# Sparse attention with an ELU MLP on one core: batch 2 transposed by the DMA crossbar, and batch 0's local P v moved ahead of its strided half

## The chip, the core and the metric

The kernel runs on one core of one Trainium2 chip. The metric is device time in microseconds (us) of one execution. "Before" names the kernel as it stood, "after" the changed one. Line numbers (L12) are those of the kernel before.

## The reference, cut to what matters

```python
# q, k, v: (8 batches, 8 heads, 576 positions, 64) f32
scores = q @ k.T / sqrt(64)
local   = (rel >= 0) & (rel < 32)                  # heads 0-3, rel = query - key
strided = (rel >= 0) & (pos_k % 32 == pos_q % 32)  # heads 4-7
attn = softmax(where(mask, scores, -1e9))          # then / (sum + 1e-9)
y = attn @ v                                       # (8, 8, 576, 64)
x = y.transpose(0, 2, 1, 3).reshape(4608, 512)
h = x @ w_in                                       # (512, 2048)
g = where(h > 0, h, exp(min(h, 0)) - 1)            # ELU
out = g @ w_out                                    # (2048, 512)
```

## The kernel before, in words

**Attention.** The eight heads of a batch are taken in four pairs: pairs 0 and 1 have the local mask, 2 and 3 the strided one. The positions are renumbered so that the strided mask falls into small blocks; each pair is worked in two halves (u = 0, 1). The steps of a pair and half have letters, which the item lists of the code use:

- T, `piece_T` (L255): transposes of q and k of the pair on TensorE into PSUM, then one copy each to SBUF (L253) on VectorE or ScalarE. The results lie in qlT and klT (local) and qsT and ksT (strided), each with two buffers, for even and odd batches.
- S, `piece_S` (L274): scores (L293), exp on ScalarE (L296), product with the mask on VectorE (L298 strided, L304 local), which gives pm.
- M, `mm_O2` (L355): the sums of pm (L368, L374) and P v (L378).
- E, `tail_O2` (L382): 1/sum as ln and exp on ScalarE (L385, L387), and the product into xT on VectorE (L313, L317). X is M and E together; O is a variant for later batches (L339).

**MLP.** The 4608 rows are taken in 18 subtiles of 256. `l1` (L397) makes hps = x w_in for two of 16 column blocks (L406), then the ELU: exp on ScalarE (L413), then two VectorE steps (L420, L421), or Relu on ScalarE and one VectorE step (L416, L417). `l1_wide` (L423) does four blocks at once (L431, L437, L439, L440). `l2` (L457) makes a quarter of a 128-row output (L463); after the fourth, ScalarE copies it out (L468) and SP stores it.

**Order.** The program is scheduled by hand: each engine runs its instructions in the order in which they are written. `spins` (L487) are idle matmuls, about 0.145 us each, that stand between TensorE's steps in the head of the kernel. The stages:

1. Batch 0's attention, with f32 loads and casts on the engines, by an item list (L530-555). The order before is: local T and S; strided transposes T2, T3; strided S4 to S7; strided M4 to M7; local M0 to M3; 12 spins. `cast_v` (L156) casts the local v; `one_columns` (L525) fills the columns of ones in vlx and vsx, on ScalarE, in two places (item "1", and after the list).
2. L1 of subtiles 0 and 1 (L576-582), first `l1_wide` (hpw), with batch 1's strided transposes T2, T3 between.
3. L2 of those subtiles, with the rest of batch 1's attention between its 16 quarters (item list L602-625, "2" is one quarter). Item "t" there transposes batch 2's strided pairs, on TensorE.
4. The main loop (L655-663): step n is one `l1` of the subtiles 2 to 17, and `l2` runs on so far that n + 10 quarters are done. The remaining attention is hung in at given n. SC[b] gives the n at which the S steps of a batch start, in the order of pairs 2, 3, 0, 1; its X or O follow 1.5 steps later. Batch 2's local transposes are at n = 8 and 10 ("TT").

From batch 3 on, the four transposes of a batch are done by DMA (`dma_T` L161, "Ts"), issued by SP, each a single instruction of all four heads, with rows padded from 72 to 80. Batches 1 and 2 are transposed on TensorE; for them `load_ql16` (L112) brings q in one DMA in a layout (qld) that is transposed in 16 pieces of 64 rows (L268) in place of 8 of 128.

**Loads.** The loads of batch 0's local q and k are issued by SP and ScalarE; all others by Pool, one after another, in the order written. `load_str` (L141) fills qs, ks or vs; these three have one buffer each, so that a load of the next batch waits until all of the previous one has been read.

Of the kernel before, what the change touches and what calls it, by code (L numbers as in the profile page):

```python
# [17 lines left out]
D = 64  # L18
HG = 4
NS = 8  # L20
RS = S // NS
LQ = 96
LB = S // LQ
PRE = STRIDE
SUB = 256
RP = 80
# [4 lines left out]
def kernel(  # L31
# [44 lines left out]
    vs = const([RS, HG, NS * D], BF16, "vs")  # L76

    qlb = [const([RP, 2, NS, 2 * D], BF16, f"qlb{i}") for i in range(2)]
    qld = [t.rearrange("p a s c -> p (a s c)").rearrange("p (h c) -> p h c", h=HG) for t in qlb]
    klb = [const([LQ, 2, LB, 2 * D], BF16, f"klb{i}") for i in range(2)]  # L80
    KLW = PRE + 2 * S
    KSW = 16 * RP + 48
# [23 lines left out]
    def load_vl(b, eng):  # L106
        x = v[b, 0:HG].rearrange("h (t p) d -> p (h t) d", p=LQ)
        t = vl32.rearrange("p a x t d -> p (a x t) d")
        eng.dma_start(out=t[PRE:128], in_=x)
        eng.dma_start(out=t[0:PRE, 1:], in_=x[LQ - PRE:, 0:HG * LB - 1, :])  # L110


    def load_ql16(b):
        if b < 3:
            nc.gpsimd.dma_start(out=qld[b % 2][0:RS],
                                in_=q[b, 0:HG].rearrange("h (p s) d -> p h (s d)", s=NS))
            return
        for h in range(HG):
            nc.gpsimd.dma_start(  # L119
                out=qlb[b % 2][0:RS, h // 2, :, (h % 2) * D:(h % 2 + 1) * D],  # L120
                in_=q[b, h].rearrange("(p s) d -> p s d", s=NS))

    def load_kl16(b):
        for h in range(HG):
            nc.gpsimd.dma_start(  # L125
                out=klb[b % 2][:, h // 2, :, (h % 2) * D:(h % 2 + 1) * D],
                in_=k[b, h].rearrange("(t p) d -> p t d", p=LQ))
# [14 lines left out]
    def load_str(b, dst, src):  # L142
        nc.gpsimd.dma_start(  # L143
            out=dst[0:RS], in_=src[b, HG:2 * HG].rearrange("h (p s) d -> p h (s d)", s=NS))
# [35 lines left out]
    ones = const([128, D], BF16, "ones")  # L180
    dist = const([RS, RS], I32, "dist")
    nc.vector.memset(warm, 1.0)  # L182
    nc.vector.memset(identity, 1.0)
    nc.vector.memset(base_l, 1.0)
    for t in (qs, ks):
# [2 lines left out]
        identity, identity, compare_op=ALU.is_equal, fill=0.0,  # L188
        base=0, pattern=[[1, 128]], channel_multiplier=-1,
    )  # L190
    load_str(0, qs, q)
    load_str(0, ks, k)
    nc.gpsimd.affine_select(
        base_l, base_l, compare_op=ALU.is_ge, fill=0.0, base=-1,
        pattern=[[-1, NS], [-NS, LQ // NS]], channel_multiplier=1)
    nc.gpsimd.affine_select(
        base_l, base_l, compare_op=ALU.is_ge, fill=0.0, base=PRE,
        pattern=[[1, NS], [NS, LQ // NS]], channel_multiplier=-1)
    load_str(0, vs, v)
    nc.gpsimd.iota(dist, pattern=[[1, RS]], base=RS, channel_multiplier=-1)  # L200
    nc.vector.memset(qlb[0][64:RP], 0.0)
    load_vl(0, nc.gpsimd)
    for i in range(2):
        nc.gpsimd.dma_start(out=w_in_sb[i],
                            in_=w_in_v[:, :, i * 1024:(i + 1) * 1024])

    nc.vector.memset(vl32[0:PRE, 0, 0, 0, :], 0.0)
    nc.vector.memset(ones, 1.0)
    for i in range(2):
        nc.vector.memset(klT[i][:, 0:PRE], 0.0)  # L210
# [20 lines left out]


    def pitch(b):
        return RS if b < 3 else RP

    def t_parts(b, hp, nm):
        i, a, n = b % 2, hp % 2, RS
        if hp >= 2:
            src = qs if nm == "q" else ks
            dst = (qsT if nm == "q" else ksT)[i][:, a * 8 * n:(a + 1) * 8 * n]  # L240
            blk = [src[0:n, 2 * a + j // 4, (j % 4) * 128:(j % 4 + 1) * 128] for j in range(8)]
        elif nm == "q":
            dst = qlT[i][:, a * 8 * n:(a + 1) * 8 * n]
            blk = ([qlb[i][0:n, a, j] for j in range(NS)] if b not in (1, 2) else
                   [[qld[i][0:n, 2 * a + x, j * D:(j + 1) * D] for x in range(2)]
                    for j in range(NS)])
        else:
            dst = klT[i][:, PRE + a * S:PRE + (a + 1) * S]
            blk = [klb[i][:, a, j] for j in range(LB)]
        return dst, blk  # L250
# [4 lines left out]
    def piece_T(b, hp, engs=None, wide=True):  # L255
        both = [t_parts(b, hp, nm) for nm in "qk"]
        if wide:
            pw = p_x.tile([128, 2, 1024], BF16, tag="x", name="tp2")
            ps = [pw[:, 0, 0:S], pw[:, 1, 0:S]]
        else:  # L260
            ps = [p_h.tile([128, S], BF16, tag="h", name="tp") for _ in range(2)]
        for i, (dst, blk) in enumerate(both):
            n = S // len(blk)
            for j, x in enumerate(blk):
                o = ps[i][:, j * n:(j + 1) * n]
                if type(x) is list:
                    for z in range(2):
                        nc.tensor.transpose(o[z * D:(z + 1) * D], x[z], identity[0:n, 0:n])  # L268
                else:
                    nc.tensor.transpose(o, x, identity[0:n, 0:n])  # L270
        for i, (dst, blk) in enumerate(both):
            copy(engs[i] if engs else nc.vector, dst, ps[i])

# [248 lines left out]
    cast_q(nc.vector, 1)  # L522
    cast_k(nc.vector, 1)
    P = [(p, u) for p in range(4) for u in range(2)]
    def one_columns(i):  # L525
        for t in (vlx[i], vsx[i]):
            o = t.rearrange("p a t (y d) -> p (a t) y d", d=D)[:, :, 1, :]
            nc.scalar.copy(o, warm[0:o.shape[0], 0:D].unsqueeze(1).to_broadcast(o.shape))

    for it in ("f7 S0 S1 1 f6 T1 f6 S2 S3 m f8 T2 T3q T3k f3 S4 S5 f3 S6 S7 M4 f3 E4 M5 f3 E5 M6 f3 E6 "  # L530
               "v M7 f3 E7 M0 f3 E0 M1 f3 E1 M2 f3 E2 M3 f12 E3").split():
        n = int(it[1:].strip("qk")) if len(it) > 1 else 0
        if it == "m":
            mask_strided()
        elif it[0] == "f":
            spins(n)
        elif it == "1":
            one_columns(0)
        elif it == "v":
            cast_v(nc.vector, 0, 0)  # L540
            cast_v(nc.gpsimd, 0, 1)
        elif it[0] == "T" and len(it) == 3:
            dst, blk = t_parts(0, n, it[2])
            ps = p_h.tile([128, S], BF16, tag="h", name="tp")
            for j, x in enumerate(blk):
                nc.tensor.transpose(ps[:, j * RS:(j + 1) * RS], x, identity[0:RS, 0:RS])
            copy(nc.vector, dst, ps)
        elif it[0] == "T":
            piece_T(0, n, (nc.vector, nc.scalar if n > 1 else nc.vector), False)
        elif it[0] == "S":  # L550
            do(("S", 0, *P[n]))
        elif it[0] == "M":
            do(("M", 0, *P[n], p_h))
        else:
            do(("E", 0, *P[n]))

    nc.vector.memset(qlb[1][64:RP], 0.0)
    nc.vector.memset(vlx[1][0:PRE, :, 0, :], 0.0)
    one_columns(1)
    load_str(1, qs, q)  # L560
    load_str(1, ks, k)

# [19 lines left out]
            l1(j, 4 * h + 3)  # L582
    load_str(2, qs, q)
    load_str(2, ks, k)
    load_kl16(2)
    load_ql16(2)
    load_vl16(2)


    L2S = [(j, kk, part) for j in range(NSUB) for kk in range(2) for part in range(4)]  # L590
# [8 lines left out]
                l2_last(j, kk)  # L599
            l2n[0] += 1  # L600

    for it in ("2 S4 2 S5 2 2 B4 S6 2 E4 A5 S7 2 E5 B6 2 E6 A7 2 E7 v "  # L602
               "T0 2 S0 S1 2 T1 k B0 2 E0 S2 2 A1 E1 S3 2 B2 E2 2 A3 2 E3 t 2 x").split():
        n = int(it[-1]) if it[-1].isdigit() else 0
        if it == "2":
            l2_to(l2n[0] + 1)
        elif it == "v":
            load_str(2, vs, v)
        elif it == "k":
            load_kl16(3)  # L610
            load_ql16(3)
            load_vsx16(3)
        elif it == "t":
            for p in (2, 3):
                piece_T(2, p)
        elif it == "x":
            load_str(3, qs, q)
            load_str(3, ks, k)
            load_vl16(3)
        elif it[0] == "T":  # L620
            piece_T(1, n, (nc.vector, nc.scalar))
        elif it[0] in "AB":
            do(("M", 1, *P[n], p_x if it[0] == "A" else p_h))
        else:
            do((it[0], 1, *P[n]))
# [3 lines left out]
    def at(n, *its):  # L629
        jobs.setdefault(int(2 * n) / 2, []).extend(its)  # L630

    def Ts(b):
        for w in ("qs", "ks", "kl", "ql"):
            dma_T(b, w)


    SC = {2: (2.5, 5.5, 9, 12), }
    SC.update({b: tuple(15 + 16 * (b - 3) + 4 * i for i in range(4)) for b in range(3, B)})
    for p, n in ((0, 8), (1, 10)):
        at(n, lambda p=p: do(("TT", 2, p)))  # L640

    for b in range(3, B):
        st = int(SC[b][0])
        if b > 3:
            at(st - 13, lambda b=b: (load_str(b, qs, q), load_str(b, ks, k), load_kl16(b),
                                     load_ql16(b), load_vsx16(b), load_vl16(b)))
        at(st - (3 if b == 3 else 4), lambda b=b: Ts(b))
    for b in range(2, B):
        for i, p in enumerate((2, 3, 0, 1)):
            for u in range(2):  # L650
# [5 lines left out]
    for n, (j, t) in enumerate(L1S):  # L656
        for f in jobs.pop(n, []):
            f()
        l2_to(n + 10)
        for f in jobs.pop(n + .5, []):  # L660
            f()
        l1(j, t, mode="B" if n < 18 and n % 3 == 0 else "A")
# [31 lines left out]
```

The softmax here doesn't subtract the row's maximum and nothing guards it: scores larger than these inputs give would overflow.

## Time and profile before

| | before |
|---|---|
| time, median of 6 runs | 324.55 us |
| lowest and highest of the 6 | 323.82 and 326.07 us |
| the profiled execution, its own time | 324.17 us |
| its span in the profile | 322.5 us |
| PE (TensorE) busy | 310.7 us, 96% of the span |
| DVE (VectorE), ACT (ScalarE), Pool busy | 239.5, 220.2, 114.9 us |
| L463, L2 matmuls | 143.6 us |
| L406, L1 matmuls | 140.7 us |

The span is the stretch from the first to the last instruction; 324.17 - 322.5 = 1.7 us of the execution lie outside it. Busy time is a sum over instructions; an engine that is busy for 96% of the span can gain by less work or by smaller gaps. The chain of waits, which the profile follows back from the last instruction, tells for each moment which engine or transfer held up the end. PE is TensorE, PEld its weight loads, SP the engine that issues stores and DMA transposes.

### The profile page before, as it was taken

Reading aid. Unit: us, or ns where it says so; the run is one execution under the profiler, and the core shown is the slowest. Engines: PE = TensorE matmul, PEld = TensorE weight load, DVE = VectorE, ACT = ScalarE, POOL = GpSimd, SP = SyncE. Lnnn points to the kernel's source line nnn. Section 1 sums busy time; section 2 is a strip of 40 time slices with the busy share of each in tenths; the row PEclk is TensorE's granted clock in tenths of the full one; section 3 lists DMA queues with packets and bytes.
Section 4 is the critical chain, followed back from the end, with each engine's and each line's share of the span. In section 5 each row is a group of like instructions: output and inputs, shape, how many; then the busy total and the mean of one; then the engine's idle time right before and its main releaser. Section 6 shows DMA issues by size and latency. Waiting matters only on the chain.

```text
span 322.5 us, 7819 instructions
## 1 busy us (share of the span) xinstructions
PE 310.7 (96%) x2992; PEld 223.9 (69%) x2992; DVE 239.5 (74%) x485; ACT 220.2 (68%) x429; POOL 114.9 (36%) x162
## 2 busy tenths in 40 slices
PE   8898998979999999999999999999999999999995
PEld 6668944567667777777777777777777777777763
DVE  7764973477667888888888888898888866666660
ACT  3787765677788788777777777778788643443431
POOL 6262376896046903491269025920000000000000
PEclk9999999999999999999999999999999999999999
DMA  7999999999199939995999499969211111111212
GB/s 169 195 208 210 207 151 139 154 149 129 34 144 181 135 54 150 180 125 79 140 172 154 62 134 169 148 77 167 59 35 35 34 35 33 34 35 48 51 33 65
DMA packets 113990, 36.36 MB, mean 113 GB/s; under 512 B 101154, under 2 KB 107458, under 8 KB 113954
## 3 DMA queue, kind: packets, MB, share of 16 engines
q0 software_dynamic: 79696, 18.87, 60.9%
q1 hardware_dynamic: 32766, 16.28, 24.2%
q10 hardware_dynamic: 1492, 0.74, 0.9%
q8 instruction: 23, 0.38, 0.5%
q14 instruction: 13, 0.11, 0.1%
HBM read 38.04 MB, written 9.44 MB: 147 GB/s over the span
## 4 chain that ended last, share of the span: by engine, by line
PE 83%; DVE 6%; ACT 4%; DMA 4%; issue 1%; SPq 0%; DVEq 0%; ACTq 0%
PE ops L463 37%; PE hps L406 33%; PE sc L293 3%; PE ox L345 3%; DMA kl<-in_k_dram 2%; DVE g L421 2%; DMA ksT<-ks 1%; DVE he L420 1%; DVE g L440 1%; PE opl L478 1%; PE idle L487 1%; PE tp L270 1%; ACT big L437 1%; ACT wr L439 1%; PE o_ps L378 1%
## 5 line engine op out<-in xcount | busy, mean ns | idle before, releaser
L463 PE MATMUL ops<-w_out_sb,g 128*128 128x512 bf16 x560 | 143.6, 380 | 0.1
L406 PE MATMUL hps<-xT,w_in_sb 128*128 128x256 bf16 x1088 | 140.7, 273 | 1.3 <-DVE g L421 1.3
L406 PEld LDWEIGHTS <-w_in_sb 128*128 128x128 bf16 x1088 | 117.3, 114 | 23.6 <-issue 1.4
L413 ACT ACTIVATE he<-hps 128x512 f32<-128x512 f32 x136 | 80.2, 592 | 52.2 <-PE hps L406 50.4
L421 DVE TENSOR_TENSOR g<-he,hps 128x512 bf16<-128x512 bf16 x130 | 89.3, 687 | 13.5
L463 PEld LDWEIGHTS <-g 128*128 128x128 bf16 x560 | 50.4, 98 | 37.2 <-DVE g L421 0.3
L420 DVE TENSOR_SCALAR he<-he 128x512 bf16<-128x512 f32 x130 | 58.0, 446 | 20.9 <-ACT he L413 19.5
L296 ACT ACTIVATE e<-sc 128x576 bf16<-128x576 f32 (+1 forms) x64 | 38.4, 645 | 4.5 <-PE sc L293 4.4
L468 ACT COPY osb<-ops 128x512 f32<-128x512 f32 x35 | 20.5, 587 | 12.4 <-PE ops L463 9.7
L143 POOL DMA_DIRECT2D qs<-in_q_dram x8 | 6.1, 761 | 50.1 <-DMA qsT<-qs 48.9
L125 POOL DMA_DIRECT2D klb<-in_k_dram x28 | 20.7, 751 | 8.6 <-DMA w_in_sb<-in_moe_w_in_dram 4.5
L348 ACT ACTIVATE ln<-ox 64x288 f32<-64x288 f32 x40 | 16.3, 408 | 10.6 <-PE ox L345 10.1
L133 POOL DMA_DIRECT2D vlx<-in_v_dram x28 | 22.0, 785 | 4.3 <-DMA w_out_sb<-in_moe_w_out_dram 2.3
L317 DVE TENSOR_TENSOR xT<-ox,rc 64x288 bf16<-64x288 f32 x40 | 18.1, 453 | 5.7 <-ACT rc L351 5.3
L313 DVE TENSOR_TENSOR xT<-ox,rc 64x288 bf16<-64x288 f32 x40 | 18.1, 453 | 5.7 <-ACT rc L351 5.4
L119 POOL DMA_DIRECT2D qlb<-in_q_dram x20 | 16.5, 831 | 13.1 <-DMA ks<-in_k_dram 9.0
L134 POOL DMA_DIRECT2D vlx<-in_v_dram x28 | 17.3, 616 | 4.9 <-DMA qs<-in_q_dram 1.6
L351 ACT ACTIVATE rc<-ln 128x288 f32<-128x288 f32 x40 | 17.7, 443 | 1.3
L349 ACT ACTIVATE ln<-ox 64x288 f32<-64x288 f32 x40 | 16.1, 403 | 0.5
L138 POOL DMA_DIRECT2D vsx<-in_v_dram x20 | 16.2, 819 | 0.0
L304 DVE TENSOR_TENSOR pm<-e,mask_l 128x576 bf16<-128x576 bf16 x32 | 13.5, 452 | 3.5 <-ACT e L296 3.1
L487 PE MATMUL idle<-warm 128*128 128x256 bf16 x92 | 14.7, 306 | 1.3 <-DVE warm L182 1.3
(101 smaller groups left out, 242.8 us busy)
## 6 DMA issues: line engine op xcount, KB each, us to landing
out_dram<-osb SPq DMA_DIRECT2D x31, 144.0 KB
qs<-in_q_dram POOLq DMA_DIRECT2D x8, 288.0 KB, 6.7
ks<-in_k_dram POOLq DMA_DIRECT2D x8, 288.0 KB, 8.4
w_in_sb<-in_moe_w_in_dram POOLq DMA_DIRECT2D x2, 1024.0 KB, 15.9
w_out_sb<-in_moe_w_out_dram POOLq DMA_DIRECT2D x4, 512.0 KB, 16.4
klb<-in_k_dram POOLq DMA_DIRECT2D x28, 72.0 KB, 8.2
vlx<-in_v_dram POOLq DMA_DIRECT2D x28, 72.0 KB, 3.8
qlb<-in_q_dram POOLq DMA_DIRECT2D x20, 72.0 KB, 7.1
```

Of the source, the lines that this page charges most:

```text
L125: nc.gpsimd.dma_start(out=klb[b % 2][:, h // 2, :, (h % 2) * D:(h % 2 + 1) * D], in_=k[b, h].rearrange("(t p) d -> p t d", p=LQ))
L133: nc.gpsimd.dma_start(out=t[PRE:128], in_=x)
L296: nc.scalar.activation(e[0:R], sc[0:R, :, 0:W], ACT.Exp, scale=scale)
L313: nc.vector.tensor_mul(xs[:, u * W:(u + 1) * W], o[pr], rc[pr])
L317: nc.vector.tensor_mul(dst, o[pr].rearrange(pat, b=3, s=NS), rc[pr].rearrange(pat, b=3, s=NS))
L406: nc.tensor.matmul(hps[:, mm], lhsT=w_in_of(m, c), rhs=xT[:, c, r0:r0 + SUB], start=(c == 0), stop=(c == KC - 1))
L413: nc.scalar.activation(e, hps, ACT.Exp)
L420: eng.tensor_scalar(e1, e, scalar1=1.0, scalar2=1.0, op0=ALU.min, op1=ALU.subtract)
L421: nc.vector.tensor_tensor(gt, e1, hps, op=ALU.max)
L463: nc.tensor.matmul(ops, lhsT=g[:, m, kk * 128:(kk + 1) * 128], rhs=w_out_sb[:, m, :], start=(m == 0), stop=(m == MC - 1))
L468: nc.scalar.copy(o_sb, ops)
L487: nc.tensor.matmul(ps, lhsT=warm[:, 0:128], rhs=warm[:, 0:ps.shape[-1]], start=True, stop=True, skip_group_check=True)
```

## The change

1. **Batch 0, head.** The fills of ones go to the very start of ScalarE's work, the two memsets of v's first rows ahead of the others on VectorE. The load of the local v is Pool's first, ahead of qs; the load of ks follows the two `affine_select`. The item list takes the local P v (M0 to M3) before the strided transposes, with `cast_v` right after `mask_strided`; the strided halves run S4 S6 S5 S7 and M4 M6 M5 M7; the tail of 12 spins and E3 is gone. There are 81 spins in place of 92.
2. **Batches 1 and 2, q.** The qld layout is gone: `load_ql16` issues four DMAs of 72 KB for every batch.
3. **Batch 2.** Its four transposes are DMA transposes on SP: qs and ks at the first "t" of the item list of stage 3, kl and ql at the second. The TT steps are gone, and `pitch` is 80 for batch 2.
4. **Batch 2, later.** SC[2] is (4.5, 7.5, 10, 12.5) in place of (2.5, 5.5, 9, 12). Three of the 16 L2 quarters of stage 3 move into the first steps of the main loop.
5. **Batch 1.** T0 goes ahead of A7, both of its copies to VectorE. Pool's loads of batch 2 (kl, ql, vl) come after that of vs, at "v"; those of batch 3 are split between "k" and "x" in another order.

The diff, without the removed definitions of `one_columns` and `Ts`, which only move:

```diff
-qld = [t.rearrange("p a s c -> p (a s c)").rearrange("p (h c) -> p h c", h=HG) for t in qlb]
...
 def load_ql16(b):
-    if b < 3:
-        nc.gpsimd.dma_start(out=qld[b % 2][0:RS],
-                            in_=q[b, 0:HG].rearrange("h (p s) d -> p h (s d)", s=NS))
-        return
     for h in range(HG):
...
 nc.vector.memset(warm, 1.0)
+nc.vector.memset(vl32[0:PRE, 0, 0, 0, :], 0.0)
+nc.vector.memset(vlx[1][0:PRE, :, 0, :], 0.0)
...
+for i in range(2):
+    one_columns(i)
+load_vl(0, nc.gpsimd)
 load_str(0, qs, q)
-load_str(0, ks, k)
 nc.gpsimd.affine_select(
...
+load_str(0, ks, k)
 load_str(0, vs, v)
 nc.gpsimd.iota(dist, pattern=[[1, RS]], base=RS, channel_multiplier=-1)
 nc.vector.memset(qlb[0][64:RP], 0.0)
-load_vl(0, nc.gpsimd)
...
 def pitch(b):
-    return RS if b < 3 else RP
+    return RS if b < 2 else RP
...
-for it in ("f7 S0 S1 1 f6 T1 f6 S2 S3 m f8 T2 T3q T3k f3 S4 S5 f3 S6 S7 M4 f3 E4 M5 f3 E5 M6 f3 E6 "
-           "v M7 f3 E7 M0 f3 E0 M1 f3 E1 M2 f3 E2 M3 f12 E3").split():
+for it in ("f7 S0 S1 f6 T1 f6 S2 S3 m v f6 M0 f3 E0 M1 f3 E1 M2 f3 E2 M3 f3 T2 E3 T3q T3k f3 S4 S6 f3 S5 S7 "
+           "M4 f3 E4 M6 f3 E6 M5 f3 E5 M7 f3 E7").split():
...
-nc.vector.memset(vlx[1][0:PRE, :, 0, :], 0.0)
-one_columns(1)
 load_str(1, qs, q)
...
 load_str(2, ks, k)
-load_kl16(2)
-load_ql16(2)
-load_vl16(2)
...
-for it in ("2 S4 2 S5 2 2 B4 S6 2 E4 A5 S7 2 E5 B6 2 E6 A7 2 E7 v "
-           "T0 2 S0 S1 2 T1 k B0 2 E0 S2 2 A1 E1 S3 2 B2 E2 2 A3 2 E3 t 2 x").split():
+for it in ("2 S4 2 S5 2 2 B4 S6 2 E4 A5 S7 2 E5 B6 2 E6 T0 2 t A7 v E7 S0 2 T1 S1 2 k B0 2 E0 S2 2 A1 E1 S3 t B2 2 "
+           "E2 A3 E3 x").split():
...
     elif it == "v":
         load_str(2, vs, v)
+        load_kl16(2)
+        load_ql16(2)
+        load_vl16(2)
     elif it == "k":
+        load_str(3, qs, q)
+        load_str(3, ks, k)
+        load_vsx16(3)
         load_kl16(3)
         load_ql16(3)
-        load_vsx16(3)
     elif it == "t":
-        for p in (2, 3):
-            piece_T(2, p)
+        Ts(2, *(("qs", "ks") if l2n[0] < 10 else ("kl", "ql")))
     elif it == "x":
-        load_str(3, qs, q)
-        load_str(3, ks, k)
         load_vl16(3)
     elif it[0] == "T":
-        piece_T(1, n, (nc.vector, nc.scalar))
+        piece_T(1, n, (nc.vector, nc.scalar if n else nc.vector))
...
-SC = {2: (2.5, 5.5, 9, 12), }
+SC = {2: (4.5, 7.5, 10, 12.5), }
...
-for p, n in ((0, 8), (1, 10)):
-    at(n, lambda p=p: do(("TT", 2, p)))
...
-    l2_to(n + 10)
+    l2_to(max(n + 10, min(13 + (n + 2) // 2, 16)))
```

More of the change, by code (lines that the diff above doesn't have):

```diff
@@ L190, with one_columns @@
     )
+    def one_columns(i):
+        for t in (vlx[i], vsx[i]):
+            o = t.rearrange("p a t (y d) -> p (a t) y d", d=D)[:, :, 1, :]
+            nc.scalar.copy(o, warm[0:o.shape[0], 0:D].unsqueeze(1).to_broadcast(o.shape))
+    for i in range(2):
+        one_columns(i)
+    load_vl(0, nc.gpsimd)
     load_str(0, qs, q)
-    load_str(0, ks, k)
     nc.gpsimd.affine_select(
@@ L205 @@
                             in_=w_in_v[:, :, i * 1024:(i + 1) * 1024])
-    nc.vector.memset(vl32[0:PRE, 0, 0, 0, :], 0.0)
     nc.vector.memset(ones, 1.0)
@@ L243, in t_parts @@
             dst = qlT[i][:, a * 8 * n:(a + 1) * 8 * n]
-            blk = ([qlb[i][0:n, a, j] for j in range(NS)] if b not in (1, 2) else
-                   [[qld[i][0:n, 2 * a + x, j * D:(j + 1) * D] for x in range(2)]
-                    for j in range(NS)])
+            blk = [qlb[i][0:n, a, j] for j in range(NS)]
         else:
@@ L265, in piece_T @@
                 o = ps[i][:, j * n:(j + 1) * n]
[L266 to L270, printed above, removed]
+                nc.tensor.transpose(o, x, identity[0:n, 0:n])
         for i, (dst, blk) in enumerate(both):
@@ L524 @@
     P = [(p, u) for p in range(4) for u in range(2)]
[L525 to L528, printed above, removed]
-    for it in ("f7 S0 S1 1 f6 T1 f6 S2 S3 m f8 T2 T3q T3k f3 S4 S5 f3 S6 S7 M4 f3 E4 M5 f3 E5 M6 f3 E6 "
-               "v M7 f3 E7 M0 f3 E0 M1 f3 E1 M2 f3 E2 M3 f12 E3").split():
+    for it in ("f7 S0 S1 f6 T1 f6 S2 S3 m v f6 M0 f3 E0 M1 f3 E1 M2 f3 E2 M3 f3 T2 E3 T3q T3k f3 S4 S6 f3 S5 S7 "
+               "M4 f3 E4 M6 f3 E6 M5 f3 E5 M7 f3 E7").split():
         n = int(it[1:].strip("qk")) if len(it) > 1 else 0
@@ L536 @@
             spins(n)
-        elif it == "1":
-            one_columns(0)
         elif it == "v":
@@ L600, in l2_to, with Ts @@
             l2n[0] += 1
-    for it in ("2 S4 2 S5 2 2 B4 S6 2 E4 A5 S7 2 E5 B6 2 E6 A7 2 E7 v "
-               "T0 2 S0 S1 2 T1 k B0 2 E0 S2 2 A1 E1 S3 2 B2 E2 2 A3 2 E3 t 2 x").split():
+    def Ts(b, *names):
+        for w in names:
+            dma_T(b, w)
+    for it in ("2 S4 2 S5 2 2 B4 S6 2 E4 A5 S7 2 E5 B6 2 E6 T0 2 t A7 v E7 S0 2 T1 S1 2 k B0 2 E0 S2 2 A1 E1 S3 t B2 2 "
+               "E2 A3 E3 x").split():
         n = int(it[-1]) if it[-1].isdigit() else 0
@@ L630, in at @@
         jobs.setdefault(int(2 * n) / 2, []).extend(its)
-    def Ts(b):
-        for w in ("qs", "ks", "kl", "ql"):
-            dma_T(b, w)
-    SC = {2: (2.5, 5.5, 9, 12), }
+    SC = {2: (4.5, 7.5, 10, 12.5), }
     SC.update({b: tuple(15 + 16 * (b - 3) + 4 * i for i in range(4)) for b in range(3, B)})
-    for p, n in ((0, 8), (1, 10)):
-        at(n, lambda p=p: do(("TT", 2, p)))
     for b in range(3, B):
@@ L646 @@
                                      load_ql16(b), load_vsx16(b), load_vl16(b)))
-        at(st - (3 if b == 3 else 4), lambda b=b: Ts(b))
+        at(st - (3 if b == 3 else 4), lambda b=b: Ts(b, "qs", "ks", "kl", "ql"))
     for b in range(2, B):
```

## The prediction

> **What bounds the kernel now.** I read the page's busy times first, then the chain of waits in two windows, then PE's waits, then the rows of the DMA transposes. The page says that PE is busy nearly always, and its DMA row (40 slices of 8.06 us) that the DMA engines are full until about 81 us, with one lull in the eleventh slice:
>
> ```profile
> span 322.5 us, 7819 instructions
> PE 310.7 (96%) x2992; PEld 223.9 (69%) x2992; DVE 239.5 (74%) x485; ACT 220.2 (68%) x429; POOL 114.9 (36%) x162
> DMA  7999999999199939995999499969211111111212
> ```
>
> So the end moves only by what PE does, or by what PE waits for. From about 88 us on PE's waits are too small to matter; all that the change can do lies before that. The chain of waits in the head (start us, duration us, what):
>
> ```profile
> 12.08 0.71 PE tp L270 x16
> ...
> 16.07 0.24 PE s_ps L368 x2
> ...
> 23.72 0.46 DVE xT L317
> 24.45 0.91 DVE qlb L557
> ...
> 26.44 1.04 ACT vsx L528
> 27.48 0.92 ACT big L437
> ...
> 29.34 1.23 DVE g L440
> ...
> 31.75 0.27 PE hps L406
> ```
>
> The reader is to see two things. The strided transposes start at 12.08 and their P v at 16.07. And the first exp of L1 (`big`) waits at 27.48 for two fills of ones, which wait for a memset on VectorE; PE stood still from 30.4 to 31.75 behind them. The chain in the middle has PE's transposes and the stalls:
>
> ```profile
> 53.65 0.65 ACT klT L253
> ...
> 54.34 0.43 PE sc L293 x12
> ...
> 63.40 1.18 PE tp L270 x32
> ...
> 71.23 0.46 DVE pm L298
> ...
> 83.73 0.38 PE tp L268 x16
> 84.11 0.36 PE tp L270 x6
> ```
>
> PE's waits from 45 to 100 us (in total, times, longest):
>
> ```profile
> PE so L368 <- DVE pm L298: 1.6, 2, 1.3
> PE sc L293 <- ACT klT L253: 1.3, 1, 1.3
> PE sc L293 <- DVE klT L253: 0.3, 1, 0.3
> ```
>
> [...] of batch 3's transposes the first two landed 4.95 and 4.64 us after issue, and the last two, with batch 4's loads beside them, 5.95 and 7.48. [...] SP itself stands in wait ahead of its transposes: five waits at L169 of 6.9 us in all are put down to L406 alone. So a transpose whose source is late holds SP, and the stores written after it. [...] the trace has 1.3 us between the first two landings and about 3 us for those beside loads[...].
>
> **The head, part by part.** The fills of ones (0.83 and 1.04 us, twice) go to ACT's start. ACT is idle there for 3.59 us, until the cast of klb at 5.68, so I cost most of them at nothing; they need warm and one 0.22 us memset, and if that came late, up to 1 us would delay the cast, which lies on the chain. They leave ACT ahead of `big`, which then follows hpw as soon as it is made.
>
> Against that stands the order. M0 to M3 need the local v. Its two loads landed at 17.18 and 17.93 as Pool's fourth and fifth; as the first I put them at 12 to 12.8, that is qs's 10.54 plus some 0.29 MB more at the page's 195 GB/s (1.5 us), and bound it by 10.5 and 14. The cast on VectorE stands behind pm of S2 and S3 and mask_strided, which ended at 13.2 before, and lasts 0.55: about 13.8 to 14.3. Four M of about 0.8 to 1.0 us each (19.86 to 22.9 before) then put the strided transposes at about 17.5, +5.5 us. By the order written, three things are behind one another after that: T2's copies, T3's PSUM buffers (three in ps_h, of which E3 holds two), and its copy on VectorE behind E3's product. From T2 to M4 it was 4.0 us; I take 5.3. M4 to M7 with spins were 3.4 and stay. So hpw, which started at 24.18, starts at 17.5 + 5.3 + 3.4 = 26.2 to 26.7: +2.3. What no longer follows, the local M's (3.1) and the spins and E3 (1.3), is already in that.
>
> From hpw to the first g (L440): before 29.34 - 24.18 = 5.16; without the fills 1.95 (hpw) + 0.92 + 0.92 + 0.1 = 3.9. So g starts at 26.4 + 3.9 = 30.3, +1.0; the 1.28 us gap of PE behind it goes. From there VectorE works without a break (29.34 to 45.02 before), so that this +1.0 is what s_ps at 45.44 sees; the cover of PE's work is not the limit there. Bounds: +0 if v lands by 10.5 and T2 follows earlier; +2.3 if hpw's delay goes through. I take **+1.2**. Pool's qs and ks land some 2 to 4 us later (before 10.54 and 12.29) and are needed at 17.5: covered by some 2 us. w_in (22.53 before) is needed at 26: covered.
>
> **The middle.** Removed from PE: 1.18 (strided, 32 transposes) and twice 0.74 (0.38 + 0.36) for the local pairs: **-2.66**. Batch 1's q in 8 transposes of 128 rows in place of 16 of 64: 0.38 against some 0.36 to 0.48, nothing. Also gone: eight copies from PSUM of 0.37 us on VectorE, which isn't the bound here except behind gaps: the 0.3 us wait for klT (-0.3). T0's copies are made before A7 and on VectorE, so the wait of 1.3 us for klT on ACT falls; something of it returns with T1, so -1.0. The waits for pm (1.6) come from L1's start, where VectorE has L417 to L421 of two steps ahead of the masks; batch 2's masks are two steps later, but so stands its own X behind them: one 1.3 us wait stays (0 saved, bounds -1.6 and +0.9). The three L2 quarters that move give PE the same work elsewhere, 0. New small stalls at T1 and M3: +0.5. Sum: -2.66 - 0.3 - 1.0 + 0.5 = **-3.4**, bounds -4.5 and -2.0.
>
> **What the crossbar costs.** Four DMA transposes and three more q loads for each of batches 1 and 2 (0.8 us of Pool each, hidden, since Pool waits for buffers there). SP's queue is moved past eight stores; they wait at most for qs and ks, which land near 56, and osb has three buffers, so nothing is taken. Batch 2's own transposes: qs and ks landed at 53.76 and 55.61 before; transposed 5 to 8 us later they are there by 59 to 64, and S at n = 4.5 needs them near 68. kl and ql load after vs, which waits for A7; I put them at 66 to 68, transposed by 71 to 76, needed near 79. Both are covered by 3 to 4 us. The load falls on batch 3: its transposes landed at
>
> ```profile
> L169 SPq DMA_TRANSPOSE ksT<-ks x4: 1637/1921/2094, 88.9 to 187.0; - x4
> ...
> PE sc L293: 0.2, 1
> ```
>
> that is, for batch 3, issued at 87.33 and 88.90, landed at 92.28 and 93.54, needed by PE at 95.73: 2.2 us in hand. The loads of batch 3 ended at 82.13, so the DMA engines had 5.2 us free before. Four more transposes take 4 x 1.3 = 5 to 4 x 3 = 12 us of them, and S of batch 3 comes 2.2 us earlier (+1.2 - 3.4). The stall is 0 if they fit, and 12 - 5.2 - 2.2 + 2.2 = 6.8 at the other end. qs and ks now load ahead of vl and vsx, which speaks for the low end: **+0.4**.
>
> **The sum,** against the profiled execution: 324.17 + 1.2 - 3.4 + 0.4 = **322.4**. That execution lies 0.4 under the median of 324.55; so the forecast is 1.8 us under it and 2.2 under the median.
>
> **Rivals.** (A, forecast) 322.4, own range 321.2 to 323.9: 38%. (B) The early v is free: it lands by 10.5, no wait is left behind E3, hpw starts no later than g needs. Then 324.17 - 3.4 + 0.4 = 321.2. For it: the gap of 1.3 us that the fills make. Against: the cast stands behind pm and the mask. 12%. (C) The gains cancel: VectorE follows hpw by the whole +2.3, and of the middle only the transposes are saved, -2.66: 324.17 + 2.3 - 2.66 + 0.4 = 324.2. For it: a stall taken away from PE often returns at the next pm. 25%. (D, the other side) The crossbar is late: the four added transposes run among loads at about 3 us each, the engines owe them until after 90 us, and S of batch 3 stands for 5.5 us: 324.17 + 1.2 - 3.4 + 5.5 = 327.5. It decides the sign from a stall of about 2.2 us, and the measurable one from 4. For it: the 5.95 and 7.48 us landings beside loads, and PE's 0.2 us wait for ksT in a later batch. Against: the free slice after 81 us. 25%.
>
> **How the numbers follow.** About 0.5%, 1.6 us, is what a measurement here can tell from no change: faster means below 322.93, slower above 326.2. A lies near that edge: 0.25 faster, 0.13 within; B 0.12 faster; C 0.24 within, 0.01 slower; D 0.01 within, 0.24 slower. Faster 0.37, same 0.38, slower 0.25. The range leaves out B's lower half and D's upper half: 321.0 to 327.6. Without D the likeliest's own range is 321.2 to 323.9.
>
> **What would show it.** T2's first transpose near 17.5 and hpw near 26.4; `big` right after hpw, no fill before it; s_ps of batch 1 near 46.6; no tp L268 anywhere; the first score of batch 3 near 93.6, with at most 0.5 us of wait for ksT. I am wrong if that wait is over 2 us, if hpw is later than 27.5, or if qsT and ksT of batch 2 hold PE near 68 us.

## The result: 1.1% slower, and the profile after

| | before | after |
|---|---|---|
| median | 324.43 us (41 runs) | 328.15 us (20 runs) |
| lowest run | 323.44 us | 325.93 us |
| profiled execution / span | 324.17 / 322.5 us | 327.51 / 325.8 us |
| mean granted TensorE clock, profiled execution | 1.000 | 0.974 |
| PE busy | 310.7 us | 312.3 us |

The ratio is 1.011, with a 95% interval of 1.0089 to 1.0131. The forecast was 322.4 with a range of 321.0 to 327.6: wrong in sign, and the time lies 0.5 us above the range. One run at 362.66 us, with a clock of 0.839, is left out of the comparison, as all disturbed runs are.

The page of after has one row that differs from before as no row of the prediction did. It is the TensorE clock that was granted, in tenths, for 40 slices of 8.1 us; before it is 9 in all of them. (Line numbers differ a little in after: hps is L403, hpw L428.)

```profile
PE   8689999989997999999999999999999999999995
...
PEclk9955999999999999999999999999999999999999
```

PE has 103 matmuls fewer and is yet busy for 1.6 us longer, because for two slices it runs at about half speed. The table by windows puts borders to it. Columns: window, its length, busy time of PE, PEld, DVE, ACT and Pool with the number of instructions, the granted clock, the DMA share and GB/s. After:

```profile
12.00:14.00 2.00, 0.07 (x2) 0.00 (x0) 1.57 (x6) 0.97 (x3) 0.41 (x1) 1.00 1.46 177
14.00:16.00 2.00, 1.84 (x26) 1.20 (x28) 0.56 (x2) 0.78 (x2) 0.78 (x1) 0.92 1.26 200
16.00:18.00 2.00, 2.00 (x21) 1.15 (x18) 0.92 (x2) 0.93 (x3) 0.00 (x0) 0.50 1.16 206
18.00:22.00 4.00, 2.72 (x37) 2.32 (x35) 0.83 (x2) 1.39 (x3) 0.20 (x1) 0.50 1.11 210
...
26.00:30.00 4.00, 4.00 (x41) 2.45 (x41) 1.48 (x4) 2.85 (x7) 0.28 (x1) 0.50 1.21 210
30.00:32.00 2.00, 2.00 (x11) 1.44 (x10) 1.37 (x2) 0.10 (x1) 2.00 (x4) 0.50 1.06 203
32.00:34.00 2.00, 2.00 (x17) 1.74 (x16) 0.00 (x0) 0.73 (x1) 1.75 (x3) 0.81 1.11 209
```

The same for before:

```profile
12.00:14.00 2.00, 1.53 (x36) 1.26 (x34) 1.85 (x8) 0.84 (x2) 0.00 (x0) 1.00 1.06 220
...
26.00:30.00 4.00, 4.00 (x39) 4.00 (x38) 0.66 (x1) 4.00 (x6) 0.96 (x2) 1.00 1.21 209
30.00:32.00 2.00, 0.71 (x8) 0.55 (x6) 1.90 (x4) 1.62 (x3) 0.92 (x2) 1.00 1.09 216
```

The reader is to see the order of things in after: from 12 to 14 us PE does next to nothing; at about 15.7 the clock goes to 0.50; there it stays to about 32.7 us, 17 us, though from 21 us on PE is by the busy count full again. Before, PE never stands so long in the head. What PE waited for in after (in total, times, longest) has the hole on its first line:

```profile
PE o_ps L375 <- DVE vlx L153: 2.1, 1, 2.1
PE sc L290 <- DMA ksT<-ks: 1.6, 1, 1.6
```

It is the wait of M0 for the cast of the local v. The chain of waits of after gives the marks that answer to those of before:

```profile
3.28 10.17 DMA vl<-in_v_dram
...
13.54 0.57 DVE vlx L153
...
18.46 0.49 PE tp L267 x8
...
30.16 3.08 PE hpw L428 x16
...
33.27 1.03 ACT big L434
...
51.94 0.31 PE s_ps L365 x2
...
92.18 7.32 DMA ksT<-ks
...
99.55 0.43 PE sc L290 x16
```

Where the 3.3 us of span went: s_ps of batch 1 is at 51.94 in place of 45.44 (+6.5). From there to the scores of batch 3, without the wait ahead of them, it is 99.55 - 1.65 - 51.94 = 45.96 in place of 95.80 - 45.44 = 50.36 (-4.4). The wait for ksT costs 1.65. The rest to the end is 226.25 in place of 226.70 (-0.45). So 6.5 - 4.4 + 1.65 - 0.45 = 3.3.

### The profile page after: what moved, and what is told of

It is laid out like the page before. It is cut to its first block, busy times and chain, and to the rows that moved or that the text cites. A ratio compares the mean times of both kernels' runs of the same rounds, so it can differ in the third digit from the quotient of the medians.

```text
span 325.8 us, 7623 instructions
## 1 busy us (share of the span) xinstructions
PE 312.3 (96%) x2889; PEld 223.6 (69%) x2889; DVE 237.1 (73%) x478; ACT 219.7 (67%) x428; POOL 121.3 (37%) x168
## 4 chain that ended last, share of the span: by engine, by line
PE 87%; DMA 5%; DVE 3%; ACT 2%; issue 1%; POOL 0%; DVEq 0%
PE ops L460 36%; PE hps L403 35%; PE sc L290 4%; PE ox L342 3%; DMA vl<-in_v_dram 3%; DMA ksT<-ks 2%; PE idle L484 2%; PE hpw L428 2%; PE tp L267 1%; PE opl L475 1%; DVE g L418 1%; PE o_ps L375 1%; PE s_ps L365 1%; ACT rc L384 0%; POOL vl L108 0%
## 5 line engine op out<-in xcount | busy, mean ns | idle before, releaser
L403 PE MATMUL hps<-xT,w_in_sb 128*128 128x256 bf16 x1088 | 140.6, 273 | 0.8 <-DVE g L418 0.5
L403 PEld LDWEIGHTS <-w_in_sb 128*128 128x128 bf16 x1088 | 117.4, 113 | 23.2 <-issue 1.2
L418 DVE TENSOR_TENSOR g<-he,hps 128x512 bf16<-128x512 bf16 x130 | 89.3, 687 | 14.3 <-DVE he L417 0.5
L114 POOL DMA_DIRECT2D qlb<-in_q_dram x28 | 23.3, 837 | 15.1 <-DMA ks<-in_k_dram 9.7
L345 ACT ACTIVATE ln<-ox 64x288 f32<-64x288 f32 x40 | 16.3, 408 | 10.7 <-PE ox L342 10.2
L129 POOL DMA_DIRECT2D vlx<-in_v_dram x28 | 17.5, 626 | 2.6 <-DMA klb<-in_k_dram 2.6
L484 PE MATMUL idle<-warm 128*128 128x256 bf16 x81 | 16.0, 350 | 1.3 <-DVE warm L177 1.3
L295 DVE TENSOR_TENSOR pm<-e,mask_s 72x576 bf16<-72x576 bf16 x32 | 13.6, 450 | 4.1 <-ACT e L293 3.9
```

The source lines that it names most:

```text
L114: nc.gpsimd.dma_start(out=qlb[b % 2][0:RS, h // 2, :, (h % 2) * D:(h % 2 + 1) * D], in_=q[b, h].rearrange("(p s) d -> p s d", s=NS))
L403: nc.tensor.matmul(hps[:, mm], lhsT=w_in_of(m, c), rhs=xT[:, c, r0:r0 + SUB], start=(c == 0), stop=(c == KC - 1))
L418: nc.vector.tensor_tensor(gt, e1, hps, op=ALU.max)
L484: nc.tensor.matmul(ps, lhsT=warm[:, 0:128], rhs=warm[:, 0:ps.shape[-1]], start=True, stop=True, skip_group_check=True)
```

## The experiments

**The theory** is that the head loses its time to the low clock: PE's hole of 2.1 us lets the clock fall, and the sparse work after it doesn't bring it back. **The rivals**: the new order of batch 0 costs it by its waits alone; or the crossbar costs it. Times before are the median of before on the same chip.

**The hole ahead of M0 filled.**

```diff
-"f7 S0 S1 f6 T1 f6 S2 S3 m v f6 M0 ..."
+"f7 S0 S1 f6 T1 f6 S2 S3 m v f20 M0 ..."
```

> The changed kernel with 20 spins in place of 6 ahead of M0, so that PE is busy while it waits for v. Theory (the clock): the 2.1 us hole lets the granted TensorE clock fall to 0.5 from 16 to 33 us; without the hole the mean clock is 1.000, hpw starts near 26.5 in place of 30.2, and the time falls by 3 to 5 us, to 323 to 325. Rival (the order itself, and the crossbar): PE waits for v with or without spins, so the time stays within 1 us of 328 and hpw at 30.

Measured: 327.19 us against 324.46 (326.41 is the median of the runs compared), ratio 1.0069 [1.0043, 1.0095]; clock of the profiled run 0.984. Neither expectation: a third of the loss or somewhat more is gone. The windows of this kernel tell why:

```profile
18.00:19.00 1.00, 0.70 (x11) 0.42 (x10) 0.49 (x2) 0.00 (x0) 0.00 (x0) 1.00 1.11 209
19.00:20.00 1.00, 0.42 (x8) 0.32 (x8) 0.26 (x1) 0.23 (x1) 0.00 (x0) 1.00 1.12 213
20.00:22.00 2.00, 1.54 (x19) 1.21 (x18) 0.77 (x3) 1.17 (x3) 0.60 (x1) 0.62 1.12 212
22.00:24.00 2.00, 2.00 (x36) 1.21 (x35) 1.04 (x4) 1.18 (x2) 2.00 (x4) 0.50 1.15 203
```

The clock now survives the first hole (cut to 1.07 us) and falls at 20.5, amid the waits between the strided transposes (0.55 and 0.73 us, with T3 waiting for T2's copies). There were more holes than one, and the first filling left them.

**The head alone,** on the kernel before. The diff is part 1 of the change, and nothing else.

> The kernel before with only the changed head (batch 0's order, its loads, the fills of ones). Theory (the clock): the hole and the low clock are there again, s_ps of batch 1 is some 6 us late, and nothing gives it back: 329 to 331. Rival (the crossbar costs the time): the head costs about 1 us, 325 to 326, with a clock near 1.000.

Measured: 330.27 us against 324.46, ratio 1.017 [1.0128, 1.0213], clock of six runs 0.969 to 0.984. The head alone costs at least as much as the whole change; the crossbar is not needed for the loss. A second profile of this same kernel (its label speaks of a filling; there is none in it):

> A second look at the kernel of e2 without timing, for its trace alone: the same as e2.

Measured: 328.51 us in one run, clock 0.988. Here the clock was at half in two spells, from 15.3 to 18.7 and from 22.1 to 25.5 us, with full speed between. The same program, nearly the same holes (2.7 us ahead of M0, 2.2 in the first profile), another length of the spell, which was 20.5 us there: so its length is not a property of the code alone. The two here are near 3.4 us.

**The middle alone:** the changed kernel with the head of before, that is, with part 1 of the change undone.

> The changed kernel with the head of before. Theory (the clock): the clock stays at 1.000 and the middle saves the 4.3 us that the trace shows between s_ps of batch 1 and the scores of batch 3, less a wait for ksT of 1.6 us or more: 321.5 to 324. Rival (the crossbar costs the time): 326 or more, with a wait for ksT of over 4 us.

Measured: 323.29 us against 324.46, ratio 0.9957 [0.9936, 0.9979], clock 1.000 in the profiled run. As the theory had it: parts 2 to 5 of the change are a gain. In the profiled run s_ps of batch 1 is at 46.18 and the scores of batch 3 at 92.95, 46.8 us apart with a wait of 0.88 us for ksT among them. But the 21 runs compared fall into two groups: 15 with a clock of 0.998 or more have a median of 322.9, and 6 at 0.995 of 324.9. A clock of 0.995 is 0.005 x 323 = 1.6 us of clock lost, or one spell of some 3.2 us at half.

**All three holes of the head filled.**

```diff
-... m v f6 M0 ... M3 f3 T2 E3 T3q T3k ...
+... m v f27 M0 ... M3 f3 T2 E3 f5 T3q T3k ...
 def piece_T(b, hp, engs=None, wide=True):
...
             n = S // len(blk)
+            if b == 0 and hp == 2 and i == 1:
+                spins(4)
```

> The changed kernel with spins in all three of the head's holes: 27 in place of 6 ahead of M0, 4 between the transposes of q and k in T2, 5 ahead of T3q. Theory (the clock): with no hole left the granted clock stays at 1.000 in nearly every run, hpw starts at 27 to 27.5 and the time is 322 to 324, so that the low clock was worth 4 to 5 us and the order itself some 2. Rival (the holes don't matter[...]): the clock still falls near 20 us, as in the first filling, and the time stays at 326 to 328.

Measured: 324.58 us against 324.66, ratio 1.0000 [0.9969, 1.0031]. Its windows in the head:

```profile
12.00:14.00 2.00, 2.00 (x21) 1.80 (x19) 1.45 (x6) 0.58 (x2) 0.00 (x0) 1.00 1.45 167
14.00:16.00 2.00, 2.00 (x27) 1.24 (x25) 0.82 (x2) 1.15 (x3) 1.20 (x1) 1.00 1.29 204
...
18.00:22.00 4.00, 3.02 (x52) 2.23 (x50) 1.64 (x4) 2.04 (x4) 1.27 (x2) 1.00 1.12 211
26.00:30.00 4.00, 4.00 (x45) 3.72 (x44) 2.08 (x4) 2.52 (x6) 2.59 (x4) 1.00 1.17 207
```

Idle matmuls alone, which compute nothing, take 328.15 to 324.58 (against before, from 1.011 to 1.0000): 3.6 us were the low clock of the head. hpw starts at 27.1, in place of 30.2. And the new order still waits for v as it did: only what PE does meanwhile has changed. 324.58 is over the 322 to 324 that I expected, and again there are two groups, 7 runs at 0.997 or more (median 323.2) and 7 lower (326.2). In the profiled run, of the second group, the clock falls not in the head but at 96.5 us, after a wait of 2.3 us for ksT ahead of batch 3's scores. That is a second place where the clock falls to 0.50 after a wait.

**Denser work in the spell.** The hole is left as it is; 24 more spins stand between the steps of the strided half.

```diff
-... T3k f3 S4 S6 f3 S5 S7 M4 f3 E4 M6 f3 E6 M5 f3 E5 M7 f3 E7
+... T3k f6 S4 S6 f6 S5 S7 M4 f9 E4 M6 f9 E6 M5 f9 E5 M7 f3 E7
```

> The changed kernel, hole and all, with 24 more spins between the steps of the strided half (S4 to M7). It asks why the clock stays at 0.5 for 17 us. Theory (density): with more of PE's time in full-size matmuls the clock comes back before hpw, within 3 to 7 us of the first added spins, near 26 us. Rival (a fixed time): it stays at 0.5 until the dense hpw again, and hpw only starts later by the spins' 6 to 7 us.

Measured: 329.64 us in one run, clock 0.979; the clock came back at about 27.5 us, having fallen at 13.9. That is within the spread of after. The same kernel, timed:

> The kernel of e6 again, timed, because one look can't tell it from the spread of the changed kernel (mean clock 0.966 to 0.984, median 0.974 in 20 runs, which is a spell at half clock of some 17 us). Theory (density brings the clock back): the median clock is 0.980 or more, a spell of 13 us or less. Rival (fixed, or set by hpw alone): the median clock is 0.974 or less, since hpw comes later.

Measured: 327.97 us against 324.67, ratio 1.0101 [1.0083, 1.0119], four runs with clocks of 0.979 to 0.990, median 0.987. Windows of its profiled run:

```profile
16.00:18.00 2.00, 2.00 (x21) 1.21 (x22) 0.91 (x2) 1.11 (x3) 0.00 (x0) 0.57 1.17 207
...
22.00:26.00 4.00, 4.00 (x46) 2.50 (x46) 1.73 (x5) 1.54 (x3) 2.41 (x4) 0.50 1.11 198
26.00:30.00 4.00, 4.00 (x54) 3.13 (x51) 1.83 (x4) 3.05 (x8) 0.00 (x0) 0.93 1.20 207
```

The clock is back at 26.5 us, ahead of hpw. So the spell is not of fixed length, and more full-size matmuls between the small steps seem to end it sooner: two of the four runs have a clock of 0.990, and no run of after is above 0.984. Four runs are few, and the small steps are not always too thin to end a spell: in e3 two ended amid them, at 18.7 and 25.5 us. The spins cost what they bring, and the time stays.

**The spins taken out of before.** The 66 spins of the item list go; the order, the loads and everything else stay.

```diff
-"f7 S0 S1 1 f6 T1 f6 S2 S3 m f8 T2 T3q T3k f3 S4 S5 f3 ... M3 f12 E3"
+"S0 S1 1 T1 S2 S3 m T2 T3q T3k S4 S5 ... M3 E3"
```

> The kernel before without the 66 spins of the head's item list (26 ahead of it stay). Theory (the clock): the holes that the spins filled let the clock fall in the head as in the changed kernel: mean clock under 0.985 and 2 to 6 us slower, 326 to 330. Rival (the clock doesn't depend on such holes, the wait for v does something of its own): PE has 9.6 us less to do in the head, and the time falls by 1 to 3 us.

Measured: 326.44 us against 324.60, ratio 1.0047 [1.0025, 1.0069], median clock 0.968. Windows of its profiled run:

```profile
10.00:12.00 2.00, 1.00 (x21) 0.67 (x19) 1.18 (x4) 1.71 (x3) 0.79 (x2) 0.51 1.41 203
...
20.00:22.00 2.00, 1.70 (x20) 1.11 (x21) 1.38 (x3) 1.81 (x5) 2.00 (x3) 0.50 1.12 210
...
26.00:28.00 2.00, 2.00 (x12) 1.41 (x10) 1.00 (x2) 0.87 (x2) 0.00 (x0) 0.50 1.19 197
```

Less work, and slower. PE comes to hpw about as early as before (24.4 us, before 24.2), but hpw runs at half clock, and the first g starts at 31.0 in place of 29.3. It needs neither the wait for v nor the new order: in the old order too, holes are enough. That is the third run that shows the clock apart from everything else in the change.

**Old order, fills first:** the middle alone, and of part 1 of the change only the fills of ones and the memset of vlx at the start.

> The changed middle, the order and loads of before in the head, and of the head's changes only the fills of ones and their memset at the start. Theory: big follows hpw with no fill ahead of it, the 1.3 us hole of PE behind it goes, and the time is 1 us under that of the middle alone: 321.5 to 322.5. Rival: VectorE's chain of the wide stage takes it up, 323.

Measured: 323.88 us against 324.66, ratio 0.9961 [0.994, 0.9983]: nothing against the middle alone, where 1 us was expected. The profiled run shows big right after hpw (26.37 after 24.59), so the gain was made in the head and lost again. PE comes to batch 3's scores earlier, and waits there 2.2 us in place of 0.9; and 11 of the 18 runs compared are at a clock of 0.995 or less (median 324.4; the other seven 322.0), in place of 6 of 21. In the profiled run itself the wait left the clock at 1.00:

```profile
91.00:92.00 1.00, 0.13 (x2) 0.00 (x0) 0.66 (x2) 0.76 (x2) 0.63 (x2) 1.00 1.74 204
92.00:93.00 1.00, 0.00 (x0) 0.00 (x0) 0.90 (x2) 0.00 (x0) 0.15 (x1) 1.00 1.59 237
93.00:94.00 1.00, 0.64 (x18) 0.47 (x19) 0.17 (x1) 0.29 (x1) 0.09 (x1) 1.00 1.95 200
```

**The load of the local v of batch 3 written behind its transposes,** on the kernel of e7.

```diff
         elif it == "x":
-            load_vl16(3)
+            at(12.5, lambda: load_vl16(3))
```

> The kernel of e7 with batch 3's load of the local v put behind its four transposes (at n = 12.5). Theory (the wait for ksT comes of loads beside the transposes): ksT lands within 5.5 us of issue in place of 6.4 to 8, the wait of 0.9 to 2 us ahead of batch 3's scores goes: 320.5 to 322. Rival (the transposes are late because SP issues them late): nothing changes.

Measured: 323.67 us against 324.66, ratio 0.9954 [0.9932, 0.9976]: the same as e7. qsT and ksT still landed 7.6 and 8.3 us after issue, and PE waited 2.4 us. But the edit moved the loads in the text of the program only. Pool issues them and SP the transposes, and in the trace Pool doesn't wait for SP: the eight loads stand beside the pair as they did, the first 0.9 us after qsT's issue (1.3 in e7) and the last 7.3 (7.8). From the timelines of SP and Pool:

```profile
84.81 2.49 SPq L164 DMA_TRANSPOSE qsT<-qs  x1
87.41 2.64 SPq L164 DMA_TRANSPOSE ksT<-ks  x1
...
85.73 0.77 POOL L128 DMA_DIRECT2D vlx<-in_v_dram  x1
...
92.14 0.59 POOL L129 DMA_DIRECT2D vlx<-in_v_dram  x1 [1.14 <-DMA qlb<-in_q_dram]
```

So this run doesn't test whether the loads of v slow the transposes; that theory stays open. The windows of this kernel show the second spell:

```profile
93.00:94.00 1.00, 0.31 (x3) 0.04 (x1) 0.48 (x2) 0.94 (x2) 0.74 (x1) 1.00 3.43 153
94.00:95.00 1.00, 0.00 (x0) 0.00 (x0) 0.90 (x2) 0.00 (x0) 0.00 (x0) 1.00 2.48 139
95.00:96.00 1.00, 0.29 (x12) 0.30 (x13) 0.20 (x1) 0.00 (x0) 0.00 (x0) 0.76 1.31 239
96.00:97.00 1.00, 1.00 (x16) 0.48 (x11) 0.15 (x1) 0.83 (x2) 0.74 (x2) 0.50 1.57 195
...
98.00:99.00 1.00, 1.00 (x7) 0.74 (x6) 0.00 (x0) 0.00 (x0) 1.00 (x2) 0.54 1.19 194
99.00:100.00 1.00, 1.00 (x9) 0.64 (x7) 0.00 (x0) 0.48 (x1) 1.00 (x3) 1.00 1.27 321
```

From 95.5 to 98.9, 3.4 us, at half: the wait of 2.4 us costs about 1.7 us more, an estimate (half of 3.4). Here, among the dense matmuls of the MLP, the spell is as short as any in these profiles.

**What the spells have in common** shows when the profiles are laid side by side. Nine spells at half clock have both ends in the windows: they last 3.4 us (e3 twice, e5, e8), 10.2 (e1, e12), 13.7 (e6), 17.1 (after) and 20.5 (e2), that is one, three, four, five and six times 3.41 us (after's 17.07, from 15.68 to 32.74 us, by five). A tenth, in e11, is at 0.50 from 10.0 us to past 28. Full speed between the two spells of e3 lasts 3.4 us too. The spells lie differently against the program from run to run: the clock falls 1.2 us into the hole ahead of M0 in e2, and 1.5 us after the end of that hole in after. Nor does the length of a wait alone tell what follows. After 2.2 us ahead of batch 3's scores in e7 the clock stayed at 1.00, after 2.4 at the same place in e8 it fell to 0.50, and amid the small matmuls of e1 it fell after waits of 0.55 and 0.73 us. What decides between them was not shown.

**Batch 3's first pair of transposes two steps of the main loop earlier,** on the kernel of e7.

```diff
-        at(st - (3 if b == 3 else 4), lambda b=b: Ts(b, "qs", "ks", "kl", "ql"))
+        if b == 3:
+            at(st - 5, lambda b=b: Ts(b, "qs", "ks"))
+            at(st - 3, lambda b=b: Ts(b, "kl", "ql"))
+        else:
+            at(st - 4, lambda b=b: Ts(b, "qs", "ks", "kl", "ql"))
```

> The kernel of e7 (old order of batch 0, fills first, new middle) with batch 3's transposes of qs and ks issued two steps earlier, at n = 10, and those of kl and ql at n = 12 as they were. Theory: their sources land near 79.4, so they can run from 80 on and land by 88 to 89; the wait of 2.2 us ahead of batch 3's scores goes, and with it the 3.4 us spell at half clock that followed it in 12 of 20 runs of e7; the median falls by 2 to 3 us to 321 to 322 and the clock is over 0.997 in nearly all runs. Rival (the DMA engines are behind, not the issue): the pair lands at 92 to 93 again and nothing changes.

Measured: 321.34 us against 324.60, ratio 0.9897 [0.9864, 0.993], and all eight runs at a clock of 0.998 or more. ksT was issued at 80.4 and landed at 90.1, 9.7 us later and over 1 us later than I expected, but ahead of need: the scores of batch 3 start without a wait for it. Of e9's timeline of PE (start, duration, instruction, idle before it and who ended it):

```profile
92.08 0.30 PE L290 MATMUL sc<-qsT,ksT 64*128 64x72 bf16 x8
92.73 0.30 PE L290 MATMUL sc<-qsT,ksT 64*128 64x72 bf16 x8 [0.35 <-DVE xT L314]
```

This version beats both kernels.

**The same on the changed order,** with its holes filled (e5).

> The changed kernel with its holes filled (as in e5) and the same earlier pair. Theory: both spells at half clock are gone; what is left against e9 is the cost of the new order of batch 0 alone, 1 to 2 us: 322 to 323.5. Rival: no change against e5, 324.5.

Measured: 322.65 us against 324.60, ratio 0.9932 [0.9904, 0.9959], all nine runs at 0.997 or more. With the clock held in both places, the new order of batch 0 is 1.3 us slower than the old one (322.65 against 321.34): hpw at 27.1 in place of 25.2, s_ps of batch 1 at 47.96 in place of 45.35, of which a part is waited away later.

## Why the prediction was wrong, point by point

- **The head, +1.2: the step that failed.** M0's wait for v was foreseen; v was put at 12 to 12.8 with a bound of 14 (13.45 measured), and its cast at 13.8 to 14.3 (14.11). What that wait does to PE was not: "Four M of about 0.8 to 1.0 us each (19.86 to 22.9 before) then put the strided transposes at about 17.5". From the third on they took 1.38 each, at half clock, and T2 came at 18.46. The durations of before were carried into a place where PE had stood still for 2 us, as if they did not depend on that. So did the rest: M4 to hpw, put at 3.4, took 5.5 (24.67 to 30.16), and hpw to the first g, put at 3.9, took 5.1. What was left out is the price of the hole: 3.6 us by e5 against after. The stages themselves were priced nearly right, as e10 shows, where the clock is held: the strided transposes at 17.9 (put at 17.5), from there to M4 5.4 (5.3), on to hpw some 3.7 (3.4, without the three spins behind M7), and to the first g 3.9 (3.9). But at s_ps of batch 1 that came to +2.5 in e10 and +1.95 in e5, where +1.2 was taken and +2.3 was the bound. A part of it is waited away later, so that 1.3 are left at the end (e10 against e9). That this lies so near the 1.2 is partly luck: resampling the 9 and 8 runs gives an estimate of 0.1 to 2.0. The row of the granted clock stood on the page and was not used: it was 9 in every slice, and I took it for a constant.
- **"The chain in the head" and its spins.** The sum counts the 11 spins that go as a gain or as nothing. e11 shows what they are for: 66 of them removed from before cost 1.8 us, with less work on PE.
- **The middle, -3.4** (its terms add to -3.46). Right in mechanism, and under its size: -4.4 in after. The transposes are gone, and the wait for klT on ACT. Between the two marks PE's waits fell from 3.2 to 2.0 us without that for ksT, 1.2 where the sum had 0.8; of the other 3.2 the sum had 2.66. Most of the last half microsecond is in batch 1's local transposes, which the prediction put at nothing: a pair takes 0.52 us for 14 transposes (56.51 in after) where before it took 0.38 + 0.36 for 22 (55.74), 0.22 less for each of two pairs.
- **The crossbar, +0.4.** Right in place, too small: 1.65 us of wait in after, 0.9 to 2.4 in the other kernels that issue the pair at the same step, and about 1.7 more, by the estimate from e8, where a spell at half clock follows (after 2.3 us in e5 and 2.4 in e8, not after 2.2 in the profile of e7). The prediction took from before that batch 3's loads end at 82.13 and leave the DMA engines 5.2 us free. In after the eight loads of its v went out from 88.9 to 93.8 us, and the last landed at 99.7: they ran beside the pair, which was issued at 89.4 and 92.2 and took 7.0 and 7.3 us from issue to landing (before 4.95 and 4.64). That these loads slowed it is not shown, since e8 left them where they were. Issuing the pair earlier mends the wait (e9).
- **Rival D** had the right sign and the wrong cause: its stall of 5.5 us didn't come; 1.65 did. B and C held neither: the early v was not free, and the gains of the middle did not cancel.
- **What would show it.** The second of the signs, "if hpw is later than 27.5" (30.16), was the one that came; ksT's wait stayed under 2 us, and batch 2's transposes held PE nowhere in after. But of the 3 to 4 us in hand that were put there, 0.7 were left (ksT landed at 73.2, its scores are at 73.95), and in e7, e8 and e9 PE waited 0.7 to 0.9 us for it.

Of the eight profiles with a hole of 2.0 to 2.7 us, seven show the clock at 0.50 behind it (after, e2, e3, e5, e6, e8, e12). Behind the hole of 2.2 us in e7, and behind that of 1.3 us in before, it stayed at 1.00. Being busy again doesn't bring it back at once: in after PE counts as full from 22 us on, and the clock stood at 0.50 to 32.7.

What stays open: which work brings the clock back. e12 points to more full-size matmuls ending the spell sooner, and doesn't tell which property of the small ones (rows, columns, or gaps that the profile doesn't see) fails to. And why the pair of batch 3 takes 7 to 10 us from issue in the changed middle was not settled: loads ran beside it in each of these kernels, and no run took them away.

## What to carry to other kernels

Before you price a wait of TensorE, ask what TensorE does meanwhile: a hole of about 2 us costs itself, and in seven of eight profiles here the clock stood at 0.50 behind it, for 3.4 to 20.5 us; the low clock of the head cost 3.6 us, for a hole of 2.1 and two smaller ones. Read the row of the granted clock even where it is constant, for TensorE's durations hold under it (three spins between two M took 0.50 us at 1.00 and 0.82 at 0.50 in after); and treat filler matmuls as part of the design, to be moved along with the waits that they cover. Where the runs of one kernel fall into two groups, look for a wait that brings the clock down in some of them; shortening the work ahead of it lengthens the wait and can undo the gain (e7), and issuing the awaited transfer earlier gives both back (e9). And look in the trace whether an edit moved what it was to move: in e8 Pool's loads, written behind SP's transposes, still went out from 0.9 us after qsT's issue.

## What the hardware showed that was not expected

- After a hole of 2.1 us the clock was at 0.50 for some 17 us in the head of after, and for 3.4 us after a wait of 2.4 us among the MLP's matmuls.
- The nine spells at half clock whose two ends the windows show last one, three, four, five or six times 3.41 us. Behind a wait of 2.2 us the clock stayed at 1.00 in one profile (e7), and behind one of 2.4 at the same place it was at 0.50 in another (e8).
- Taking 66 matmuls away made the kernel slower: ratio 1.0047 [1.0025, 1.0069].
- The strided DMA transposes of batch 3 landed 4.6 and 5.0 us after issue in before, 7.0 and 7.3 in after; those of batch 2, in the midst of the loads, took 9.8 and 11.7 there, and the issue of ksT, 2.1 us in before, took up to 4.6.
